# Two attention blocks on one core: x's columns for v requested half a set sooner and apart from their parts, sums kept open longer, some exponentials 1024 wide

## The chip, the cores and the metric

The kernel runs on one core of a Trainium2 chip. The metric is the device time of one execution in microseconds (us); lower is better. The runs of the kernel before gave 1745.47 us in the median (1745.34 to 1747.84, three runs).

## The reference, cut to what matters

Both halves take x (2048 x 640), wqkv (640 x 1920) and wo (640 x 640), all float32, with 32 heads of 20. A is a sliding window of 8 keys with a stride of 2; B is full attention. The outputs stand side by side.

```python
def _A_ref(x, wqkv, wo):                     # W, dil = 8, 2
    qkv = (x @ wqkv).reshape(B, S, 3, H, Dh).transpose(2, 0, 3, 1, 4)
    q, k, v = qkv[0], qkv[1], qkv[2]
    idx = arange(S)[:, None] - arange(W)[None, :] * dil
    ...
    attn = softmax(where(mask, einsum("bhsd,bhswd->bhsw", q, kg) * scale, -1e9))
    o = einsum("bhsw,bhswd->bhsd", attn, vg)
    return o.transpose(0, 2, 1, 3).reshape(B, S, D) @ wo

def _B_ref(x, wqkv, wo):
    ...
    p = softmax(einsum("bhqd,bhkd->bhqk", q, k) * Dh ** -0.5)
    o = einsum("bhqk,bhkd->bhqd", p, v)
    return o.transpose(0, 2, 1, 3).reshape(B, S, D) @ wo
```

## The kernel before, in words

**Numbers in two parts.** Products in fp32r keep fewer bits, so a value that enters one is cut into a first part (a rounded copy, `hi`) and a second part (value minus first part, `lo`), and a product is made of three passes (`PASSES`). `split` asks for the raw value by a DMA on SP's queue and makes both parts some ticks later: the copy on ScalarE, the difference on VectorE or, with `second=gp`, on GpSimd. A tick is a step of the program text (`tick`); `after(n, fn)` puts an instruction n ticks later into the queues. All queues run in program order.

**The stages.** First the projections of A to q and k (up to about 220 us), then those of B (up to about 281 us); both are stored in DRAM. Then the stage for v: 15 blocks and a remainder. Set c = 0 to 3 are 512 columns of A's x, c = 4 to 7 of B's; block 2c + half multiplies set c by one half of wv. From block 2 on, a matmul uses 64 rows, two run side by side, and after each pair of rows a `v_tick` follows, which also issues one `b_max` (two maxima 1024 wide) of B, loads of bq, and work of A's attention on GpSimd. `x_load(c + 2, 4)` at the end of block (c, 1) asks for the set after next and makes its parts four ticks later; `x_load(1, 5)` stands behind the first v group of block 0. `w_load` does the same for B's wv. Results go through ScalarE's copies to `ro` (four buffers) and by DMA to va_d, or to vb_d for B.

**The main loop.** B is cut into 32 units u (8 groups of 4 heads, 4 query quarters) of 16 key blocks each, 512 steps i. A step holds four halves of scores S (key rows against 512 queries), whose exponentials ScalarE makes from PSUM to SBUF (`s_exp`), four halves of maxima for a later step on VectorE, and the product of v with the exponentials (`b_pv`). The order is written out by hand in the string `ORDER`: a letter is a token, the digits its PSUM banks (eight banks of 128 x 512):

- S: two halves of scores, an exponential each. M: two halves of maxima, one reduction 1024 wide over two neighbouring banks. N: the same with two reductions of 512. Y: one half of scores and one of maxima.
- V: the product of step i - 2, with a digit if it opens a bank for the sum. Before, a sum covers two steps: the first V opens it, the second closes it. ScalarE then copies the sum to SBUF, and from the second sum of a unit on GpSimd adds the copy (`more`) to the unit's total (`braw`). The four buffers of `more` are the two tiles `spare`.
- H: a piece of A's output projection in two banks; j: a transpose of A's output on VectorE.

A's attention runs on GpSimd beside all this (`a_work`), paced by an estimate of GpSimd's time. The last 24 steps (`TAIL`) and B's output projection follow the loop.

The two lines that the change to the sums turns on are these:

```python
        n, part = divmod(kb, 2)
        ...
                      start=(part == 0), stop=(part == 1))
```

Of the kernel before, what the change touches and what calls it, by code (L numbers as in the profile page):

```python
# [75 lines left out]
def attention_pair(ctx, tc, xa, wqk_a, wv_a, wo_a, xb, wqk_b, wv_b, wo_b, oa, ob):  # L76
# [648 lines left out]
    accs, raws, spare = {}, {}, []  # L725
# [29 lines left out]
    def b_pv(i):  # L755
        u, kb = divmod(i, NKB)
        g, qc = divmod(u, NQC)
        n, part = divmod(kb, 2)
# [22 lines left out]
    def b_two(what, ns, one):  # L781
# [36 lines left out]
    def take(kind):  # L818

        m = None  # L820
        if kind == "S":
# [14 lines left out]
    def b_token(kind, ns):  # L836

        what, m = take(kind)
        b_two(what, ns if len(ns) == 2 else (ns[0], ns[0] + 1), kind == "M")
# [85 lines left out]
    def x_load(c, w):  # L925

        x, pieces = x_pieces((xa, xb)[c // 4], c % 4, gp)
        XV.append((x, pieces))
        wait[0] = w
        for fn in pieces:  # L930
            fn()
# [8 lines left out]
    for block in range(15):  # L940
        c, half = divmod(block, 2)
        s0 = c % 4 * 4
        if block < 2:
            for s in range(s0, s0 + 4):
                v_group(c, half, s)
                v_tick(2.2, False)
                if (block, s) == (0, 0):
                    x_load(1, 5)
        else:
            ps4 = [bank() for _ in range(4)]  # L950
            for second in range(2):
                for u in range(2):
# [45 lines left out]
    def begin(i):  # L998
# [29 lines left out]
        "Y07M1S36Y54V0Y71S26M4Y03V7Y06M4S31Y72V0Y13M4S76VY71M2S64S05N17V6Y04M2S51VY70M4S13S26N07V1Y25S04N36VY07S25M3Y61"  # L1028
        "V0Y72M3S56VY75M1Y63S04V5Y06M1S74VY07S64M1Y35V0Y74S16Y23VM4S73Y61V2jY70M4S31VY07Y63M4S12S70Y63jV1jS72jM4Y03VM6"
        "S52Y40V3Y71jM5S24VY70M1S46S35Y07V4S31jM6Y52VY03S71Y65jM3S02Y57V1jM3S06Y72VjM3S05Y26V7Y01M3jS56VY05M1S36Y47V5"  # L1030
        "Y03M1S64VY07S64S31N25Y70V6jM4S32M0VS75M3S26jY01jV7jY25M3S61VY02S65M3jS71V0Y26M3S75VY71Y26H54Y30H54S71H54Y62H54"
        "Y73H54M1Y06V3Y74M1S05VY07M4S61Y23V7Y60S15N42VN06S51H43Y27H43Y05H43Y61Y27H43H43M5Y01V2Y73S04M5VY70M3Y15S62V0Y17"
        "M3S62VY71M5S24Y30V1Y27M5S43VY07H23N46S15H23Y70H23Y14H23Y56H23M0Y74V5S63M0Y72VS63Y74N01V2Y36S05Y74VM0S36Y54V7"
        "Y03M1S64VN06S53H42Y71H42Y05H42Y36Y71H42Y05H42Y36V7Y02M4S63VS06M2Y14V7M5S03Y21VM3S05Y62V1Y07M3S25VY07M5S42H31"
        "H31Y07H31Y24Y56H31Y07H31M4S26V0Y71S23M4VY71M2S46Y50V1Y74S26N35VY07S62M3H51H51Y07H51Y62M3H51Y07H51N62V0S17M3S56"
        "VM1S75Y43V6Y70S51M2VY70S15M2Y46V0S71jM2Y54VS71jY26S35N40V7jN64S21Y03VM5S42Y10V3jY47M5jS02VY70M1S64S53N07V6Y52"
        "S01M3VY70M1S53S46N07V5Y41M2S06VY70Y61S42Y35S07Y61N45V2Y01M3S75VY07S16M3S52N07V1S63M4Y02VY73S04M5Y21V7Y03M5S42V"
        "Y04M2S15Y76V0S15M2Y74VS15Y76Y23V0Y14S56N73VY71Y24H56Y03H56S71H56N42S03H56H56N74S01V2Y37M5S04VY70S13M5Y42V0Y17"
        "S63N54VY71M5S23Y40V1Y72S36N54VY07M5S23Y41V7Y02S63N54VN06S51H23Y74H23Y05H23Y16Y74H23Y05H23Y16V7Y02M4S63VY06S13"
        "M4Y27V6S01jM4S32jVjM0S75Y43V2jY01M6S35jVS01M3S57N62V0S13S45M6VM1S34Y76V5Y03S21N46VY70M2S14S65N07V1Y26S03M4VY07"  # L1040
        "M2S64S51N70V6Y52M3S71VY70M1Y53S46Y07V5Y64M1S03VY07M3S62S51Y07V6Y52S43N71VY70M4S32Y16V0Y73M4S21VY73M1S64H50H50"
        "Y73H50Y46Y12H50Y73H50S41N62V7Y06S53Y42VM5S03Y21V4Y05M6S31VS05M2Y71S64V0M2S75Y16VM2S74Y56V1Y07M2S46VY07S64M2Y51"
        "V7Y06M2S45VY06M4S13H27H27Y60H27N13S45H27Y60H27S14N53V6Y75M1S03VY70S54M1Y36V0S75jM1jS43jVjM6S51Y24V3jY07M5S14V"
        "Y70M1S46S53N07V4Y56M1S03VY07M5S31S42N70V3S41M5S72VM0S74Y56V2Y73M0S46VY73S45M0S62N37V4Y05S36M1VY07M5S31S42N70V3"
        "Y41M5S72VY70M1S46S35N07V4S36M1S05VM6S03Y21V5Y04M6S13VY04M1S73H65H65Y04H65N73S21H65Y40H65S72N13V4Y05M6S31VY05"
        "S32M6Y14V5Y03S67Y21VM3S07Y61V2Y03M4S17VY03S16M4Y72V3Y01M4S67VS02M6S15Y43V0M6S12Y35VM6S14H52Y30H52Y16Y74H52Y30"
        "H52Y16H52M3Y70V1S25M6Y43VY02M6S54Y31V0Y24M6S53VY15M3S27Y06V5jS12jM3jS70jVM1S67Y34V0jY12M5S74VY71M2S46Y50V1Y74"
        "M2S65VY07M5S42S31N70V4Y35M6S21VY05M1S37S64N50V3Y27S16M4VY70M1S64S35N07V6Y41M2S05VS70M4S13Y26V7Y01M4S63VY06S12"
        "Y35Y47Y60N15V2S70S34N16VM0S73Y65V4Y70M1S35VY07S63M1H54H54Y07H54Y63Y21H54Y07H54M2S61V0Y74S56M2VY71S64M2S50V1M6"
        "S24Y35VM6S02Y54V3Y07M1S46VN07S64H51Y23H51Y06H51Y74Y23H51H51M6Y04V2Y31S07M5VY01M3S75Y62V1Y07M3S56VS07M5S24Y31V0"  # L1050
        "M5S72Y14VM5S72Y34V1jY07S26M4VjY07M2S64S51jY70jV6jM2S54Y01VM2S74Y50V1Y27M3S06VY07S62M3S51N70V6Y52M3S71VY70M1S53"
        "S46N07V5Y41M2S06VY70Y61M2S45Y07V6Y51M2S04VY70Y15S42M6S03N15V4Y07S62Y31VM6Y05S12V3S40M6Y51VS02M6S54Y13V0Y72S65"
        "M3VY71Y62H34Y50H34S71H34N26S50H34H34M1S75V6Y04M1S73VY70S54M1Y36V0Y75Y14S23VM6S51Y24V3Y07M5S14VY70S12M5Y43V0Y71"
        "M5S24VY71M2S46H50H50Y17H50Y64Y32H50Y17H50M3Y62V1S07M5Y43VY07M5S42Y31V0Y72M5S43VY74M1S36Y05V4Y37M1S60VM6S05S31j"
        "Y24jV0jM6S53Y14VY75M2jS61jV4Y05M6S32VY05M2S17S46N50V1Y72M4S36VY07M2S64S51Y07V6Y52M3S71VN70S52M3S16Y75V0Y12M3"
        "S67VY12M6S53S40Y21V5M6S41Y03VM6S41Y23V0Y74M5S13VY71M3S25S60N17V2Y36M4S01VY07S16S35N42N70V1S26Y34Y75VY02Y36H45"
        "H45Y72H45Y60Y31H45Y72H45S06N31V7Y52M3S01VS06M1S35Y47V0M1S36Y75VY14S23M5V7Y04S12M5VY04S13M5S27V4M0S35Y62VN70S15"
        "H23H23M6S41H23Y05H23H23M6N41S05V2S03M6Y54VS03Y15S76N24V0Y15M2S74VY71S65M2V4jY70S61M2VjY07M5S13S24jY70V1jM5S23"
        "Y04VjM5S72Y34V0Y17S26Y54VM1S73Y46V5Y70M1S63VY07S64M1S35N70V6Y14M2S75VY70M4S13S26N07V1Y25M3S06VY07Y62S53S41Y70"
        "N62V5Y60S43M1VY07M1S36Y45Y70V3Y42S15M6VY04M1S57Y63V4Y50M1S76VY07M5S31Y24V7Y03S61N52VY06S15M3H27H27Y60H27N15S34"  # L1060
        "H27Y60H27S13M4V6S70M1S54VY70M1S35V4Y07S63M1VY07S65M1Y34V7Y06S51M2VY06M4S13Y27V6Y01M4S32VY70M2S14H56H56Y70H56"
        "Y41Y23H56Y70H56M1Y43V7S06M4Y12VY06S15M3Y27V0S16jM3Y52VS71jM3S56Y20V7jM3S51Y06VjM3S52Y16V0Y75M3jS26VY71S26M3Y50"
        "V1Y27S63M4VY07M2S64S51N70V6Y52M3S71VS70M1S53Y46V7Y05M1S36VY03S45Y61Y27Y30N41V5S06S72M3VM0S76Y43V2Y70S15N36VY70"
# [123 lines left out]
```

## Time and profile before

| what | value |
|---|---|
| median of the runs | 1745.47 us |
| profiled execution, its own time | 1745.1 us |
| span of its instructions | 1742.9 us |
| granted TensorE clock, mean | 0.998 |
| busy PE / VectorE / ScalarE / GpSimd | 1726.1 / 1349.3 / 1337.3 / 1271.9 us |
| v stage, about | 281 to 463 us |
| main loop, about | 463 to 1628 us |

Busy time of an engine is the union of its instructions. ScalarE's and VectorE's instructions overlap their neighbours a little, so the mean length of one times the count is more than the busy time. In a row of the timeline, the first number is the start, the second the length of all the instructions merged in it (their count stands behind x), and square brackets give the idle time of the engine ahead of it and what ended that.

### The profile page before, as it was taken

The page shows a single profiled execution, that of the slowest core. Times are in us where ns is not written, and L with a number is a line of the kernel's source. Part 1 is how long each engine was busy: PE and PEld are TensorE (multiplying, and loading weights), DVE is VectorE, ACT ScalarE, POOL GpSimd, SP SyncE. Part 2 cuts the span into 40 slices and gives each one's busy share as a digit, 9 for nine tenths or more (in the row PEclk, how much of TensorE's full clock was granted, in tenths as well). Part 3 has the DMA queues.
Part 4 walks back from the last instruction along what each step waited for, and adds up shares of the span by engine and source line. Part 5 has one row for each costly group of instructions (what it writes and reads, how often), then busy time and mean ns, then how long its engine had stood idle before and what let it go on. Part 6 is the DMA issues. An engine that isn't in the chain of part 4 may idle for free.

```text
span 1742.9 us, 34666 instructions
## 1 busy us (share of the span) xinstructions
PE 1726.1 (99%) x12711; PEld 1011.2 (58%) x12711; DVE 1349.3 (77%) x1818; ACT 1337.3 (77%) x2658; POOL 1271.9 (73%) x1125
## 2 busy tenths in 40 slices
PE   9999999999999999999999999999999999999999
PEld 8988888989635544444444443444444445444568
DVE  3113232888899999999999999999999999999300
ACT  4323223232599999999999999999999999999981
POOL 0000950999899999999999999999999953545242
PEclk9999999999999999999999999999999999999999
DMA  6447878657754263445435433543642532111123
GB/s 226 120 139 242 304 258 261 219 183 219 207 152 133 91 175 119 130 127 148 128 121 158 141 126 106 176 136 110 168 137 96 142 90 55 43 36 52 34 75 113
DMA packets 194435, 248.29 MB, mean 142 GB/s; under 512 B 89308, under 2 KB 114396, under 8 KB 193272
## 3 DMA queue, kind: packets, MB, share of 16 engines
q1 hardware_dynamic: 193688, 245.41, 46.6%
q8 instruction: 100, 1.64, 0.4%
q14 instruction: 71, 0.58, 0.1%
q10 hardware_dynamic: 576, 0.66, 0.1%
HBM read 181.08 MB, written 64.91 MB: 141 GB/s over the span
## 4 chain that ended last, share of the span: by engine, by line
PE 73%; POOL 17%; DMA 4%; issue 3%; DVE 2%; ACT 1%; SPq 1%; POOLq 0%; ACTq 0%; DVEq 0%
PE ps_st L71 73%; POOL akv L71 9%; POOL braw L71 4%; DVE mx L71 2%; POOL ao L71 1%; DMA stg<-xa 1%; SPq L71 1%; DMA mdr<-mtr 1%; DMA bq<-qb_d 1%; POOL ww L71 1%; POOL al L71 1%; ACT e L71 1%; DMA s_d<-braw 1%; POOL xn L71 0%; DMA s_d<-sm 0%
## 5 line engine op out<-in xcount | busy, mean ns | idle before, releaser
L71 DVE TENSOR_REDUCE mx<-ps_st 128x1 f32<-128x512 f32 (+1 forms) x1500 | 1227.5, 877 | 72.5 <-PE ps_st L71 61.4
L71 ACT ACTIVATE e<-ps_st 128x512 f32<-128x512 f32 x2048 | 1067.3, 630 | 32.5 <-PE ps_st L71 19.6
L71 PE MATMUL ps_st<-bk,bq 60*128 60x512 f32 x2048 | 555.1, 436 | 0.5 <-DVE mx L71 0.4
L71 PE MATMUL ps_st<-bq,bk 62*128 62x512 f32 x2048 | 548.7, 431 | 3.5 <-ACT e L71 1.8
L71 PE MATMUL ps_st<-e,vb 128*32 128x512 f32 x4096 | 543.1, 604 | 0.5
L71 PEld LDWEIGHTS ps_st<-bq,bk 62*128 62x128 f32 x2048 | 276.6, 184 | 401.6 <-ACT e L71 250.2
L71 POOL TENSOR_TENSOR braw<-braw,more 128x512 f32<-128x512 f32 x224 | 288.3, 1287 | 85.6 <-ACT more L71 85.1
L71 PEld LDWEIGHTS ps_st<-bk,bq 60*128 60x128 f32 x2048 | 257.9, 184 | 102.9 <-DVE mx L71 45.1
L71 POOL TENSOR_TENSOR akv<-akv,aq 128x1280 f32<-128x1280 f32 x64 | 188.4, 2944 | 166.4 <-DMA akv<-ka_d 166.3
L71 POOL TENSOR_TENSOR akv<-akv 128x640 f32<-128x640 f32 (+3 forms) x304 | 282.6, 930 | 14.7
L71 ACT COPY ro<-ps_st 128x320 f32<-128x320 f32 (+2 forms) x172 | 73.9, 465 | 185.9 <-PE ps_st L71 104.0
L71 PE MATMUL ps_st<-ww,xn 64*128 64x320 f32 (+1 forms) x1776 | 188.1, 311 | 6.5 <-POOL xn L71 2.4
L71 PEld LDWEIGHTS ps_st<-ww,xn 64*128 64x128 f32 (+1 forms) x1776 | 175.6, 187 | 22.6 <-ACT e L71 8.3
L71 PEld LDWEIGHTS ps_st<-e,vb 128*32 128x32 f32 x4096 | 82.2, 108 | 149.9 <-issue 77.1
L71 POOL TENSOR_TENSOR akv<-akv,al 128x1280 f32<-128x1280 f32 x64 | 151.6, 2368 | 0.1
L71 ACT COPY more<-ps_st 128x512 f32<-128x512 f32 x224 | 136.7, 610 | 4.0 <-POOL braw L71 2.0
L71 PE MATMUL ps_st<-xn,w 128*128 128x512 f32 x480 | 115.8, 390 | 0.0
L71 PEld LDWEIGHTS ps_st<-xn,w 128*128 128x128 f32 x480 | 90.1, 188 | 19.4
L71 POOL TENSOR_TENSOR xn<-stg,xn 128x512 fp32r<-128x512 f32 (+1 forms) x30 | 53.8, 1804 | 62.8 <-ACT xn L71 61.5
L71 PE MATMUL ps_st<-ww,aot 64*128 64x320 f32 x960 | 99.2, 308 | 0.0
L71 ACT CAST pr<-ps_st 128x512 fp32r<-128x512 f32 x40 | 23.5, 587 | 98.7 <-PE ps_st L71 93.0
L71 PEld LDWEIGHTS ps_st<-ww,aot 64*128 64x128 f32 x960 | 91.0, 186 | 4.6 <-DVE mx L71 0.5
(65 smaller groups left out, 1042.3 us busy)
## 6 DMA issues: line engine op xcount, KB each, us to landing
akv<-ka_d SPq DMA_DIRECT2D x128, 320.0 KB
akv<-va_d SPq DMA_DIRECT2D x128, 320.0 KB
kb_d<-pr SPq DMA_DIRECT2D x20, 512.0 KB
qb_d<-pr SPq DMA_DIRECT2D x20, 512.0 KB
bk<-kb_d SPq DMA_DIRECT2D x16, 640.0 KB
bq<-qb_d SPq DMA_DIRECT2D x64, 160.0 KB
stg<-xb SPq DMA_DIRECT2D x16, 512.0 KB
rb<-s_d SPq DMA_DIRECT2D x128, 64.0 KB
```

The source lines that it names most:

```text
L71: return self.tc.keep_in_program_order(op(*a, **k))
```

## The change

What it does:

1. `x_load` is cut in two. `x_raw(c)` only asks for the three raw pieces, into buffers of the ring `p`; `x_parts(c, raws, second)` makes the parts at once. `x_raw(1)` is issued in the last pair of projections of B, behind the fourth load of bq; its parts are made behind the fourth v group of block 0, with the second parts on VectorE, and `x_raw(2)` follows there. The later sets are requested after the first tick of block (c, 1) and cut into parts at its end.
2. `w_load(0, 9)` becomes `w_load(0, 8)`.
3. `load_out(wo_a, ...)` makes its second parts on VectorE; those of wo_b stay on GpSimd.
4. In `ORDER` two letters are new. v is a V that leaves the sum open, so that a sum can cover one to five steps. T is an S whose two exponentials are one instruction over two neighbouring banks. The whole string is another one: 330 S, 254 T, 784 Y, 409 M, 119 N (before 627 S, 698 Y, 444 M, 127 N), and 225 sums are closed in it (before 243). H, j and the steps are as many as before.

```diff
+    def x_raw(c):
+        out = []
+        for a, b in PAIRS:
+            t = sb.tile([128, 1024], F32, tag="p", bufs=PB, name="stg")
+            raw = t[:, :(b - a) * 512].rearrange("p (k c) -> p k c", c=512)
+            sp.dma_start(raw, (xa, xb)[c // 4][a * 128:b * 128, c % 4 * 512:c % 4 * 512 + 512].rearrange("(k p) c -> p k c", p=128))
+            out.append((a, b, raw))
+        return out
...
                     elif g8 == 6:
                         for _ in range(4):
                             q_loads.pop(0)()
+                        xraw = x_raw(1)
...
-    def b_pv(i):
+    def b_pv(i, keep=False):
...
-        n, part = divmod(kb, 2)
+        part = int(u in accs)
...
-                      start=(part == 0), stop=(part == 1))
+                      start=(part == 0), stop=not keep)
...
-        if part == 0:
+        if keep:
             return
         del accs[u]
+        n = sums[u] = sums.get(u, -1) + 1
...
-            if kind == "s":
+            if kind == "s" and not one:
                 s_exp(i, j, r, psb[:, n])
-            elif not one or r == 1:
+            elif kind == "s" and r == 1:
+                s_exp(i, j, slice(0, 2), psb[:, n - 1:n + 1])
+            elif kind == "m" and (not one or r == 1):
...
-    def x_load(c, w):
...
+    def x_parts(c, raws, second=gp):
+        t = columns(c % 4)
+        XV.append((t, None))
+        for a, b, raw in raws:
+            u, m = t[a // (KC - 1)], a % (KC - 1)
+            hi, lo = (u[:, x, m:m + b - a] for x in range(2))
+            act.copy(hi, raw)
+            second.tensor_tensor(lo, raw, hi.bitcast(F32), ALU.subtract)
...
-                if (block, s) == (0, 0):
-                    x_load(1, 5)
+                if (block, s) == (0, 3):
+                    x_parts(1, xraw, dve)
+                    xraw = x_raw(2)
...
                     v_tick(V_US)
+                    if half and c < 6 and not second and not u:
+                        xraw = x_raw(c + 2)
...
-            w_load(0, 9)
+            w_load(0, 8)
         if half:
             if c < 6:
-                x_load(c + 2, 4)
+                x_parts(c + 2, xraw)
...
-            w, more = wide_pieces(src[h], gp)
+            w, more = wide_pieces(src[h], *((dve, gp.tensor_copy) if src is wo_a else (gp,)))
...
-        "Y07M1S36Y54V0Y71S26M4Y03V7Y06M4S31Y72V0Y13M4S76VY71M2S64S05N17V6Y04M2S51VY70M4S13S26N07V1Y25S04N36VY07S25M3Y61"
+        "Y07M1Y36N54V0Y71M5M2S04V7Y06T2M4Y71v0Y26M4S73VY71M2S64Y05Y17v6Y02M3S51VY70M1S53N46S07v5S03M1S47vY60M3T1VY07M1"
...
-                b_pv(i - LAG)
+                b_pv(i - LAG, kind == "v")
...
-            b_pv(i - LAG - 1)
+            b_pv(i - LAG - 1, True)
             b_pv(i - LAG)
```

More of the change, by code (lines that the diff above doesn't have):

```diff
@@ L724, in attention_pair @@
     P = {}
-    accs, raws, spare = {}, {}, []
+    accs, raws, sums, spare = {}, {}, {}, []
     def s_matmul(i, pl, r, p):
@@ L820, in take @@
         m = None
-        if kind == "S":
+        if kind in "ST":
             what = [s_half(), s_half()]
@@ L838, in b_token @@
         what, m = take(kind)
-        b_two(what, ns if len(ns) == 2 else (ns[0], ns[0] + 1), kind == "M")
+        b_two(what, ns if len(ns) == 2 else (ns[0], ns[0] + 1), kind in "MT")
         if m:
@@ L923, in v_tick @@
         a_pace(v_us[0])
-    def x_load(c, w):
[L927 to L931, printed above, removed]
+    def x_parts(c, raws, second=gp):
[6 more added lines that the diff above has]
+            second.tensor_tensor(lo, raw, hi.bitcast(F32), ALU.subtract)
     def w_load(half, w):
@@ new lines, in attention_pair @@
+        "S02v1S04Y56Y72vY06T4M2VY07M4Y63T1v7Y06S54M1VjY06T4M1jS37jv0jT4jM1Y36VY75M1T3Y60V7Y53Y42H16Y07H16S53N42H16S07"
+        "H16Y54H16M2Y07v4Y56M2S01VY07M5T2Y14v7Y03T5M1VY03Y46T1N57v3Y04S56M1VY07H65Y41M2H65S70H65Y41H65H65M2Y70Y14v6T2"
+        "Y75N01VS25Y74N03v6T4M1S70vjT4jM1jS73jvjY05S74M1VY70T4M1Y36V0Y75Y41H23Y60H23Y75H23Y41H23Y07H23M4Y61V0Y72S36Y54"
+        "N01v7S62M3Y05VY61S02M3Y57v6Y02S13M4VY70H12N35S46H12Y07H12Y34H12M5Y07H12V3Y04M5Y71T2v4Y07S56M2VY70T5M2Y14v0M5"
+        "Y73T1VN74T5T1N30V7M5T3Y21v0Y73M5S42VY71S24H35N06H35S71H35Y02H35Y46H35M1Y07V6Y53M1Y04T6v5Y03S21M6VY04M2T6Y15v4"
@@ L1088, in attention_pair @@
+        "v7Y14T5M2VY04Y15T2M6Y40v1Y25T6M3VY02M6S53S41N20v5Y46M2S71VY07Y61T2M4Y70v6Y13M4S72VY70M2S14S56N07v1Y25M3S06VY07"
+        "Y62T3Y51Y70v6N41T2Y05vY74T2N01VY70S52M3S16N07v5Y41M2S06VY70Y61T2M4Y07v6Y13M4S02VY70Y13T4Y62N07v1Y25T3Y06vY72T3"
+        "M5VY07M3S25S61N70v2Y36M4S71VY07Y16T4Y32Y70v1N26T4Y03vY27T4N06VY07Y25T3Y61v7Y05T1N34VN03S65T1Y47N06v3S72Y01M4V"
+        "Y72M0Y64Y53S72v6S75M0Y24VY75M0S23S46N75v2Y01T3Y76vY01T3Y56vY01T3M6VM0T3M6S52")
     owed = []
@@ L1095, in attention_pair @@
     i = 0
-    for kind, *ns in re.findall("[A-Zj][0-7]*", ORDER):
+    for kind, *ns in re.findall("[A-Zjv][0-7]*", ORDER):
         ns = [int(n) for n in ns]
@@ L1102, in attention_pair @@
             out_owed()
-        elif kind != "V":
+        elif kind not in "Vv":
             b_token(kind, ns)
```

107 lines of the change are left out of this document (48 added, 59 removed).

## The prediction, made before the changed kernel ran

> **What bounds the kernel now.** I read the page's span first, then windows by stage, then the waits of PE's weight loads in the main loop, and last the timeline around the places where PE stood. A row of the windows has the stretch and its length, the busy time and instruction count of PE, PEld, DVE, ACT and POOL, the granted clock, the DMA share and GB/s.
>
> ```profile
> span 1742.9 us, 34666 instructions
> ```
>
> ```profile
> 298.70:305.90 7.20, 2.62 (x18) 1.79 (x16) 0.00 (x0) 3.49 (x6) 4.75 (x3) 0.75 0.80 285
> 305.90:309.00 3.10, 3.10 (x20) 2.93 (x22) 0.13 (x1) 0.00 (x0) 2.94 (x5) 0.50 0.95 335
> 463.00:1628.00 1165.00, 1160.53 (x8624) 528.20 (x8624) 1133.05 (x1584) 1130.19 (x2266) 1014.78 (x895) 1.00 0.42 119
> ```
>
> ```profile
> PEld ps_st L71 <- ACT e L71: 335.9, 537, 2.8
> PEld ps_st L71 <- DVE mx L71: 160.5, 334, 0.9
> PEld ps_st L71 <- issue: 88.3, 284, 0.8
> ```
>
> In the main loop (463 to 1628 us: nearly all exponentials, most maxima and products with v) PE is busy 1160.53 of 1165 us, but that is not proof of a bound: matmuls overlap, and one that runs late is still drawn as running. VectorE is busy 1133.05 us there and ScalarE 1130.19, 97% each. VectorE's idle 31.95 us is the most that a better order alone can win. Of the 584.7 us that weight loads waited in the three rows, 335.9 (57%) ended with an exponential and 160.5 (27%) with a maximum. So ScalarE and VectorE hold the loop together, and ScalarE is more often the one that releases PE. The other place is 298.7 to 309: PE is busy 2.62 of 7.20 us, and then works at clock 0.50.
>
> **The change, part by part.** The sum is made against the profiled execution: span 1742.9, execution 1745.1 us, which is 0.4 under the median 1745.47 of the runs.
>
> (1) The second set of x's columns (c = 1) is asked for behind the fourth load of bq, in the last projection for q and k, and not after the first v group; its second parts go from GpSimd to VectorE. The chain, ScalarE, PE and VectorE of before at this place:
>
> ```profile
> 279.71 11.17 DMA bq<-qb_d
> ...
> 290.92 6.25 DMA stg<-xa
> ```
>
> ```profile
> 299.70 0.43 ACT L71 COPY ro<-ps_st 128x320 f32<-128x320 f32 x1 [4.90 <-DMA va_d<-ro]
> 300.02 1.99 ACT L71 CAST xn<-stg 128x1024 fp32r<-128x1024 f32 x2
> ```
>
> ```profile
> 298.31 0.60 PE L71 MATMUL ps_st<-ww,xl 128*128 128x320 f32 x3
> 301.12 0.41 PE L71 MATMUL ps_st<-ww,xn 64*128 64x320 f32 x2 [2.21 <-ACT xn L71]
> 303.56 1.97 PE L71 MATMUL ps_st<-ww,xn 64*128 64x320 f32 x12 [2.02 <-POOL xn L71]
> 305.87 1.70 PE L71 MATMUL ps_st<-ww,xn 64*128 64x320 f32 x10 [0.35 <-POOL xn L71]
> ...
> 309.03 1.96 PE L71 MATMUL ps_st<-ww,xn 64*128 64x320 f32 x24
> ```
>
> ```profile
> 308.87 2.36 DVE L71 TENSOR_REDUCE mx<-ps_st 128x2 f32<-128x1024 f32 x2 [20.08 <-PE ps_st L71]
> ```
>
> And a tick (one call of v_tick and the v matmuls ahead of it) in the regular course, with the place of part (3) behind it:
>
> ```profile
> 368.49 1.92 PE L71 MATMUL ps_st<-ww,xn 64*128 64x320 f32 x24
> ...
> 371.21 0.46 PE L71 MATMUL ps_st<-ww,xn 64*128 64x320 f32 x4
> 372.90 1.14 PE L71 MATMUL ps_st<-ww,xn 64*128 64x320 f32 x12 [1.23 <-POOL ww L71]
> ...
> 376.02 1.92 PE L71 MATMUL ps_st<-ww,xn 64*128 64x320 f32 x24
> ```
>
> Block 1 ends at 298.31 + 0.60 = 298.91 and the second tick of block 2 begins at 309.03: 10.1 us for a tick that costs 371.21 - 368.49 = 2.7. So 7.4 us are lost: 2.21 wait for x's first parts from ScalarE, 2.02 and 0.35 for the second parts from GpSimd, and the rest because PE runs at 0.50 afterwards. The request now stands right behind the loads of bq that begin at 279.71, some 9 us before 290.92. If x lands even at 295.5, the casts (two in 1.99 us and a smaller one) and VectorE's parts end by about 299, an estimate; VectorE stood idle for 20.08 us here, so its work costs nothing. Late next are ScalarE's copies to ro: each needs a buffer that a store to va_d must free (4.90 us of waiting at 299.70), those stores now stand behind x in SP's queue, and block 2 needs all four banks that the copies of block 1 free. I leave half of 4.90, 2.4 us, to them and take **-5.0**. Ends: -7.4, and +2.4 (two further waits of 4.90 in place of the 7.4).
> [...]
>
> (2) Sets 2 to 7 are asked for three ticks ahead of the end of a set, and cut into parts at that end and not a block (four ticks) later. Three ticks are 8 us; x took 6.25 to land. The parts are the same work, one block earlier.
>
> ```profile
> 357.47 0.76 ACT L71 COPY ro<-ps_st 128x320 f32<-128x320 f32 x2 [7.39 <-issue]
> ```
>
> ScalarE stands for 7.39 us between copies in these blocks, which hides its casts; GpSimd's order changes, its work doesn't. If a set is still on its way, ScalarE stands in front of the copies that free banks, and SP's stores to va_d and loads of akv stand behind the request: bounds 0 and a late landing of 2 us (8 against 6.25 and as much again) for one set. I take **0**.
>
> (3) wv_b's first half is cut a tick sooner, and x's parts no longer lie right ahead of it on GpSimd:
>
> ```profile
> 371.31 3.88 POOL L71 TENSOR_TENSOR ww<-stg,ww 128x640 fp32r<-128x640 f32 x3
> ```
>
> PE waited 1.23 us for ww, and its tick from 371.21 took 4.8 where 2.7 is regular. GpSimd reached ww only at 371.31; one tick sooner and without x's parts ahead it has at least 2.7 us to spare for PE's first need. I take **-2.1**; ends -2.1 and 0, if GpSimd's other work fills the place.
>
> (4) wo_a's six second parts go from GpSimd to VectorE.
>
> ```profile
> 286.83 1.96 DVE L71 TENSOR_TENSOR ww<-stg,ww 128x640 fp32r<-128x640 f32 x3 [3.79 <-ACT ww L71]
> ```
>
> ```profile
> 490.49 0.58 ACT L71 COPY more<-ps_st 128x512 f32<-128x512 f32 x1 [1.98 <-POOL braw L71]
> ...
> 491.63 0.50 PE L71 MATMUL ps_st<-bq,bk 62*128 62x512 f32 x1 [1.85 <-ACT e L71]
> ```
>
> Three such parts took VectorE 1.96, so six 3.9. GpSimd, late with ww and then braw, held ScalarE's copy 1.98 us and PE through it 1.85; that goes (-1.9). VectorE has 3% idle to hide 3.9, so I put half on the path. Together **0**; ends -1.9 and +2.0.
>
> (5) The order. Counting its letters: pairs of exponentials go from 627 S to 330 S and 254 T (one exponential of 1024); maxima from 444 M, 127 N and 698 Y to 409, 119 and 784; closed sums from 243 to 225. PE's matmuls stay the same in number.
>
> ```profile
> L71 ACT ACTIVATE e<-ps_st 128x512 f32<-128x512 f32 x2048 | 1067.3, 630 | 32.5 <-PE ps_st L71 19.6
> L71 DVE TENSOR_REDUCE mx<-ps_st 128x2 f32<-128x1024 f32 x548 | 661.8, 1216 | 44.8 <-PE ps_st L71 42.7
> L71 DVE TENSOR_REDUCE mx<-ps_st 128x1 f32<-128x512 f32 x952 | 615.0, 682 | 27.7 <-PE ps_st L71 18.7
> ...
> L71 ACT COPY more<-ps_st 128x512 f32<-128x512 f32 x224 | 136.7, 610 | 4.0 <-POOL braw L71 2.0 <-PE ps_st L71 1.5 <-issue 0.3
> ...
> L71 ACT CAST xn<-stg 128x1024 fp32r<-128x1024 f32 x30 | 30.7, 1053 | 4.5 <-DMA stg<-xa 4.2 <-DMA stg<-xb 0.3
> ```
>
> ```profile
> 700.82 3.11 ACT L71 ACTIVATE e<-ps_st 128x512 f32<-128x512 f32 x6
> ```
>
> ScalarE: 18 copies fewer at 136.7 / 224 = 0.61 are 11 us. An exponential of 1024 is not in this trace. Alone, by the cast of that width, it takes 1053 ns against twice 630: 0.207 us less. In a run of six the starts lie (3.11 - 0.63) / 5 = 0.50 apart and in a run of two casts 1.99 - 1.05 = 0.94: 0.06 less than two exponentials. The exponentials do run in rows, but from PSUM, so I take half of the nearer end, 0.03 each: 8 us for 254 (ends 0 and 53). ScalarE gains 19, and PE sees its 57%: -11. VectorE: 35 M fewer at 661.8 / 548 = 1.208 against 70 halves more (86 Y, less 16 of N) at 615.0 / 952 = 0.646: +2.9, in full on the path. Banks: a T frees its first bank at 1.053 and not at 0.630, 0.42 later. By the letters the banks of a T are asked for again after 4.47 tokens on average, those of an S before after 4.21; a token of the loop lasts 1165 / 1896 = 0.61, which gives 0.16 back. The other 0.26, 254 times, is 66 us of 8 x 1165 bank-us, under 1%; I price it at +2. GpSimd's 18 adds less are hidden, since it held PE only in (4). The loop: -11 + 2.9 + 2 = **-6**. Ends: -25 (VectorE's idle 31.95 less its 2.9 and 3.9 of work) and +21 (rival E).
>
> [...]
>
> Sum: 1745.1 - 5.0 - 2.1 + 0 + 0 - 6 = **1732**.
>
> **The rivals.**
> A, the forecast: 1732, its own range 1726 to 1738.
> B: a T saves what one alone shows, and the order turns that into time until VectorE's work is the floor: -25 for -6, so 1713, or 1720 with a third of it left. For it: 57% of the waits end with ScalarE. Against: rows of exponentials show only 0.06.
> C: the request for x does not do its work, because it queues behind the loads of bk and bq (the bq of 279.71 took 11.17 us to land): (1) is 0, and the time 1737.
> D: VectorE alone sets the loop. ScalarE's relief is then worth nothing, and VectorE's 2.9 and the 2.0 of (4) are paid: 1745.1 - 7.1 + 2.9 + 2.0 = 1743, with 1739 to 1747. For it: VectorE is as full as ScalarE. Against: PE waits for it half as often.
> E, slower: banks that a T returns late stop PE. All first banks together come 254 x 0.42 = 107 us later; if a fifth of that is on the path, the loop is +21 and not -6, with -7.1 before it 1759; with an eighth (13 us) 1751. It decides from (7.1 + 3.5) / 107, one T in ten, if nothing of ScalarE's relief arrives. For it: 41% of the tokens of S, T, Y, M and N (38% before) stand in an open sum, with seven banks left. Against: the longer distance in the letters.
>
> **How the numbers follow.** A 0.38, B 0.13, C 0.11, D 0.17, E 0.21. A change of less than 0.2% (3.5 us) can't be told from none here. Faster (under 1742.0) are A, B, C and a third of D: 0.68. The same (to 1749.0): most of D, 0.10. Slower: E and a rest of D, 0.22. The range leaves out half of B and half of E: 1716 to 1753.
>
> **What would show it.** (1) is right if PE no longer waits for ACT xn or POOL xn around 299 to 309 and the clock stays at 1.00; wrong if such a wait stays, or if ACT ro waits over 5 us for va_d. (3): no PE wait for POOL ww. (4): no ACT more behind POOL braw near 490. (5): ScalarE some 20 us less busy in the loop, VectorE within 8 of 1133, an exponential of 1024 near 1.05 and its successor 0.95 later. The prediction is wrong towards B if VectorE idles under 15 us in the loop; towards D if ScalarE is relieved and the loop still takes 1165; towards E if PE's waits that end with ACT e grow.

## The result and the profile after

The changed kernel takes 1769.38 us in the median (1769.19 to 1771.7), beside 1746.26 for the kernel before on the same chip: a ratio of 1.0134, 95% interval 1.0117 to 1.0152. It is 23 us slower where 13 us faster was forecast, and 10 us above the slowest time that any case of the prediction named (1759). Its profiled execution took 1771.7 us. Numbers in brackets, (1) to (5), are the steps of the prediction.

The rows that answer to those of the prediction: the span, the windows of the two places and of the loop (stretch, length, busy time of PE, PEld, DVE, ACT, POOL, granted clock, DMA share, GB/s), then the waits of PE's weight loads in the loop, then the two shapes of exponentials.

```profile
span 1769.9 us, 34595 instructions
```

```profile
298.70:305.90 7.20, 6.21 (x73) 5.75 (x75) 2.64 (x4) 1.28 (x3) 0.00 (x0) 1.00 0.85 245
472.10:485.75 13.65, 5.61 (x24) 1.52 (x24) 6.97 (x9) 2.28 (x4) 5.37 (x9) 0.50 0.68 212
526.70:533.50 6.80, 6.61 (x27) 1.89 (x27) 3.33 (x5) 4.89 (x10) 6.57 (x5) 0.50 0.63 190
465.80:1655.50 1189.70, 1166.57 (x8626) 515.09 (x8624) 1138.00 (x1623) 1115.03 (x1997) 982.15 (x867) 0.99 0.41 116
```

```profile
PEld ps_st L71 <- ACT e L71: 315.0, 492, 0.9
PEld ps_st L71 <- DVE mx L71: 179.7, 354, 10.4
```

```profile
L71 ACT ACTIVATE e<-ps_st 128x512 f32<-128x512 f32 x1540 | 831.0, 614 | 47.1 <-PE ps_st L71 38.1 <-ACT e L71 0.3
...
L71 ACT ACTIVATE e<-ps_st 128x1024 f32<-128x1024 f32 x254 | 263.5, 1039 | 14.0 <-PE ps_st L71 12.7 <-ACT e L71 0.2
```

The first place is mended: PE is busy 6.21 of 7.20 us from 298.7 (2.62 before), at clock 1.00. ScalarE is relieved too: its busy time over the whole span falls from 1337.3 to 1321.4. And yet the loop takes 24.7 us more: from the first product of v with the exponentials to that of step 486 it lasts from 465.8 to 1655.5, 1189.7 us, and from 463.0 to 1628.0, 1165.0 us, before. The v stage ends 2.8 us later instead of sooner, and what follows the loop is 0.5 shorter: 2.8 + 24.7 - 0.5 = 27.0, the difference of the spans (1769.9 - 1742.9). These are the profiled executions; the medians lie 23 us apart.

The loop does not lose evenly. PE stands in a few places, and the waits tell of it: the longest wait for DVE mx is 10.4 us (last number of its row), where it was 0.9. The first is at 470, in the timeline of after (start, length, engine, operation, and in brackets the idle time ahead and its end):

```profile
459.02 0.33 SPq L71 DMA_DIRECT2D stg<-wo_a  x1
...
476.24 0.72 POOL L71 CAST ww<-stg 128x640 fp32r<-128x640 f32 x1 [3.82 <-DMA stg<-wo_a]
...
476.99 0.82 DVE L71 TENSOR_TENSOR ww<-stg,ww 128x640 fp32r<-128x640 f32 x1 [7.61 <-POOL ww L71]
...
480.14 0.79 PE L71 MATMUL ps_st<-bq,bk 62*128 62x512 f32 x1 [9.97 <-DVE mx L71]
```

Read it from the end. PE stands 9.97 us for maxima that free its banks. VectorE runs four of them in a row at 479.41, and none sooner: ahead of them in its queue stands a difference for wo_a, which waits 7.61 us for its first part on GpSimd, which waits 3.82 us for wo_a. This piece was asked for at 459.02 and landed just before 476.24, some 17 us later. Nothing in the loop needs wo_a yet. From 472.10, while PE still stands, its clock is at 0.50, for 13.65 us.

The second kind is at 524 and at 956:

```profile
524.96 1.26 POOL L71 TENSOR_TENSOR braw<-braw,more 128x512 f32<-128x512 f32 x1
...
526.25 0.58 ACT L71 COPY more<-ps_st 128x512 f32<-128x512 f32 x1 [2.65 <-POOL braw L71]
...
526.89 1.29 PE L71 MATMUL ps_st<-bk,bq 60*128 60x512 f32 x3 [2.31 <-ACT more L71]
```

```profile
956.75 0.58 ACT L71 COPY more<-ps_st 128x512 f32<-128x512 f32 x1 [4.94 <-POOL braw L71]
...
957.39 0.79 PE L71 MATMUL ps_st<-bq,bk 62*128 62x512 f32 x1 [4.51 <-ACT more L71]
```

ScalarE's copy `more` waits until GpSimd has read the previous copy out of the same buffer (it begins when the add at 524.96 is over), and all exponentials stand behind that copy. `spare` has four buffers, but they are chosen by the number of the sum within its unit, and begin anew with each unit. Before, every unit had eight sums and so seven copies, and a buffer came round after three copies or more. Now the letters give units of 6 to 9 sums. Where a unit has six there are five copies, and the last one and the first one of the next unit fall on the same buffer. That happens three times; the third of these stops, at 879, took 1.15 us.

The later end of the v stage has a stop of its own, at 329. VectorE waits for GpSimd's `al`, which A's softmax needs, and PE's maxima stand behind that:

```profile
330.59 0.58 DVE L71 TENSOR_REDUCE am<-al 128x32 f32<-128x256 f32 x1 [4.47 <-POOL al L71]
...
332.37 0.80 PE L71 MATMUL ps_st<-bk,bq 60*128 60x512 f32 x2 [3.45 <-DVE mx L71]
```

### The profile page after: what moved, and what is told of

The parts are those of the page before. It is cut to its first block, busy times and chain, and to the rows that moved or that the text cites. A ratio compares the mean times of both kernels' runs of the same rounds, so it can differ in the third digit from the quotient of the medians.

```text
span 1769.9 us, 34595 instructions
## 1 busy us (share of the span) xinstructions
PE 1733.3 (98%) x12711; PEld 998.6 (56%) x12711; DVE 1358.8 (77%) x1862; ACT 1321.4 (75%) x2386; POOL 1238.6 (70%) x1098
## 4 chain that ended last, share of the span: by engine, by line
PE 81%; POOL 7%; DVE 6%; DMA 4%; issue 1%; SPq 0%; ACT 0%; POOLq 0%; ACTq 0%
PE ps_st L71 81%; DVE mx L71 6%; POOL akv L71 4%; POOL braw L71 1%; DMA bq<-qb_d 1%; DMA va_d<-ro 1%; DMA stg<-wo_a 1%; POOL ao L71 1%; DMA bk<-kb_d 1%; POOL xn L71 0%; SPq L71 0%; POOL ww L71 0%; POOL al L71 0%; DMA stg<-xa 0%; DVE am L71 0%
## 5 line engine op out<-in xcount | busy, mean ns | idle before, releaser
L71 ACT ACTIVATE e<-ps_st 128x512 f32<-128x512 f32 (+1 forms) x1794 | 1049.6, 674 | 61.1 <-PE ps_st L71 50.7
L71 PE MATMUL ps_st<-bq,bk 62*128 62x512 f32 x2048 | 560.1, 436 | 18.1 <-DVE mx L71 11.1
L71 PE MATMUL ps_st<-bk,bq 60*128 60x512 f32 x2048 | 569.3, 437 | 7.6 <-DVE mx L71 4.8
L71 PEld LDWEIGHTS ps_st<-bq,bk 62*128 62x128 f32 x2048 | 270.0, 185 | 447.9 <-ACT e L71 249.9
L71 POOL TENSOR_TENSOR braw<-braw,more 128x512 f32<-128x512 f32 x206 | 265.1, 1287 | 108.8 <-ACT more L71 107.8
L71 PEld LDWEIGHTS ps_st<-bk,bq 60*128 60x128 f32 x2048 | 267.0, 185 | 87.6 <-DVE mx L71 35.5
L71 ACT COPY more<-ps_st 128x512 f32<-128x512 f32 x206 | 123.2, 598 | 14.8 <-POOL braw L71 9.7
L71 PE MATMUL ps_st<-ww,aot 64*128 64x320 f32 x960 | 103.5, 313 | 0.2 <-DVE mx L71 0.2
L71 POOL TENSOR_TENSOR xn<-stg,xn 128x512 fp32r<-128x512 f32 (+1 forms) x28 | 49.1, 1763 | 67.3 <-PE ps_st L71 66.0
```

Source lines behind the costliest of these rows:

```text
L71: return self.tc.keep_in_program_order(op(*a, **k))
```

## The experiments

Two theories. **S**: the loss is a few stalls, instructions that wait at the head of a queue which others need, and each has a place in the text from which it can be moved; without them the order is worth something like what was forecast. **O**: the new order itself is slower (banks, or VectorE's halves), and the stalls are a minor part. A time in brackets is the kernel before on the same chip; each ratio is against that.

**The three parts of the change, taken back one at a time, then together.**

e1_wo_gp, in the changed kernel:

```diff
+    gq = InOrder(tc, nc.gpsimd)
-  *((dve, gp.tensor_copy) if src is wo_a else (gp,))
+  *((gq, gp.tensor_copy) if src is wo_a else (gp,))
```

(gq is GpSimd without its pacing estimate.)

> Part (4) alone undone: wo_a's six differences are GpSimd's again, all else as in the changed kernel (GpSimd's pacing estimate too). Theory S (VectorE's program order: a difference that waits for wo_a's landing stands ahead of maxima): PE's stop of 9.97 us at 470 goes, and with it the 13.65 us at half clock, a loss of some 11 to 13 us in all: 1757 to 1759 us. Theory O (the new order itself is slower, through 1024 wide exponentials and long sums): the stop was only drawn in one place, the time stays within 4 us of 1769.4.

e2_ring, in the changed kernel:

```diff
-            more = spare[n % 2][:, n // 2 % 2]
+            mores[0] += 1
+            more = spare[mores[0] % 2][:, mores[0] // 2 % 2]
```

> The four buffers of more are taken in turn over all units, not by the number of the sum within its unit; all else as in the changed kernel. Theory S: with units of six sums the old rule takes the same buffer for two copies in a row (three times in the string), and ScalarE's copy, and PE behind it, waits for GpSimd's addition: PE's stops of 2.3, 1.15 and 4.5 us at 524, 878 and 952 and two falls of the clock go, 8 to 12 us: 1757 to 1761. Theory O: GpSimd's lag is the same, the stops move to other sums, the time stays within 4 us of 1769.4.

e3_x_old puts `x_load` back with its places, and `w_load(0, 9)`; the rest stays.

> Parts (1), (2) and (3) undone: x's columns are asked for and cut as before the change, wv_b too. Theory S: the loop of the changed kernel began 2.9 us later than before in spite of the wait for x that went; with the old course it begins near 463, so about 3 us less: 1765 to 1768. If asking sooner were a gain and the later start came from GpSimd alone, the time rises by up to 5.

e4_all3 has all three edits: of the change only the order, with T and the longer sums, is left.

> All three together: the parts (1) to (4) as before the change, the buffers of more in turn, and only the order with v and T left of the change. Theory S: the three losses add up and the order is worth nothing or a few us: 1740 to 1747. Theory O: the order costs 10 us or more by itself: 1755 or above.

Measured: e1 took 1763.13 (1745.66), ratio 1.0102 (1.0087 to 1.0117); e2 1758.54, 1.0078 (1.0063 to 1.0093); e3 1768.34, 1.0136 (1.0121 to 1.0151); e4 1750.31, 1.0031 (1.0018 to 1.0044). Against after that is -6.2, -10.8, -1.0 (which lies within the intervals) and -19.1. The two stalls are 17 of the 23 us, as S says. e2's time lies in the range that S gave it. But e1 gave half of what S expected, and its trace says why. The stop at 470 is gone, GpSimd has six differences more to do, and so comes later to the add that the copy waits for:

```profile
516.87 0.59 ACT L71 COPY more<-ps_st 128x512 f32<-128x512 f32 x1 [5.42 <-POOL braw L71]
...
517.50 1.29 PE L71 MATMUL ps_st<-bk,bq 60*128 60x512 f32 x3 [5.06 <-ACT more L71]
```

The stop that took 2.31 us in after takes 5.06 here: a part of what was mended came back through the other fault. In e2 the waits of that copy for GpSimd over the whole span fall as they should; the first row is after's, the second e2's (engine and tile, what was waited for: us in total, times, longest):

```profile
ACT more L71 <- POOL braw L71: 9.7, 4, 4.9
```

```profile
ACT more L71 <- POOL braw L71: 0.5, 1, 0.5
```

e4, though, is still 4.6 us slower than before, between S (to 1747) and O (from 1755), so the order, freed of the two, does not bring its 6.

**Wide exponentials.** e5_count is e4 with wo_a wholly as before, so that GpSimd's pacing (`gp`) counts its six differences again:

```diff
-  *((gq, gp.tensor_copy) if src is wo_a else (gp,))
+  gp
```

> As e4 (only the order with v and T is left, the buffers of more in turn), but wo_a's differences on GpSimd are counted in its pacing estimate, as before the change, so that A's attention is put into the queues some 8 us later. Theory S (what e4 still lost, 5 to 8 us around 514 to 525, was GpSimd running behind the order at the loop's start): 1742 to 1747. Theory O (the order costs the 4.6 us of e4 by itself): 1749 to 1752.

e6_count_s is e5 with a T made as two exponentials of 512:

```diff
-            if kind == "s" and not one:
+            if kind == "s":
                 s_exp(i, j, r, psb[:, n])
-            elif kind == "s" and r == 1:
-                s_exp(i, j, slice(0, 2), psb[:, n - 1:n + 1])
```

> As e5, with each T made as two exponentials of 512 (an S): banks, sums and order the same. The prediction's step (5) gave a T 0.03 us of ScalarE's time and 2 us in all for later banks: by it this one is 2 to 4 us slower than e5. Rival E (a T's banks come back too late): this one is faster than e5 by 3 us or more. If neither matters: within 2 us.

e5 took 1761.22 (1746.53), 1.0087 (1.0073 to 1.0101); e6 1766.12, 1.0115 (1.0100 to 1.0131). e6 against e5: the wide exponentials save 4.9 us. From step 32 on, the windows of e5 and then e6 are 4.7 us apart, and ScalarE is busy 12.4 us less:

```profile
548.86:1638.33 1089.47, 1081.01 (x8039) 478.60 (x8037) 1054.99 (x1496) 1037.07 (x1857) 914.60 (x805) 1.00 0.40 114
```

```profile
552.18:1646.39 1094.21, 1086.73 (x8039) 487.70 (x8037) 1056.19 (x1496) 1049.52 (x2092) 915.48 (x804) 1.00 0.40 114
```

The rival by which T's late banks cost more than T saves is refuted: with T off, the kernel is slower. e5 itself missed both theories, 10.9 us above e4 with nothing changed but an estimate in the text. Its trace has two stops, each set by a wait of VectorE for GpSimd:

```profile
521.94 0.31 DVE L71 STREAM_TRANSPOSE turn<-ao 128x128 f32<-128x128 f32 x1 [6.28 <-POOL ao L71]
...
522.88 0.79 PE L71 MATMUL ps_st<-bq,bk 62*128 62x512 f32 x1 [6.32 <-DVE mx L71]
```

```profile
1294.87 0.59 DVE L71 TENSOR_REDUCE am<-al 128x32 f32<-128x256 f32 x1 [4.98 <-POOL al L71]
...
1296.11 1.94 PE L71 MATMUL ps_st<-e,vb 128*32 128x512 f32 x8 [5.67 <-DVE mx L71]
```

They are of the same kind as the one at 470: VectorE's transpose `turn`, or its maximum `am` for A's softmax, stands ahead of B's maxima and waits for GpSimd's `ao` or `al`. In e4 the first is there with 2.32 us and the second is not.

**The stage for v on the two orders.** e7_xnew is e5 with the requests and parts of x and wv as in the change.

> As e5, with x's columns and wv_b as in the changed kernel (parts 1 to 3). The prediction gave them -7.1 us. Theory S (the earlier parts stand ahead of A's attention in GpSimd's queue, VectorE and PE then wait for a softmax): 1 to 4 us slower than e5.

e7 took 1747.45 (1746.53), 1.0008 (0.9999 to 1.0017): not a little slower than e5, as was expected, but 13.8 us faster. Its loop begins 3.3 us later than e5's (466.8 against 463.5), and the wait of `turn` there is 2.02 us and not 6.28. A loop that starts later seems to give GpSimd time. That was not tested by itself, but it is plain that the parts of the change don't add up.

To see each part without this, three kernels are the kernel **before** with one edit. e8_b_wo has wo_a's differences on VectorE alone, with the pacing kept as it was; e9_b_x1 part (1) alone (the early request for set 1, its second parts on VectorE); e10_b_xnew parts (1) to (3).

```diff
 e8   -  w, more = wide_pieces(src[h], gp)
      +  w, more = wide_pieces(src[h], *((dq, gp.tensor_copy) if src is wo_a else (gp,)))
 e9   +  xraw = x_raw(1)                  # in the last projections of B
      -  x_load(1, 5)
      +  x_parts(1, xraw, dve)            # behind the fourth group of block 0
 e10  as e9, and
      +  xraw = x_raw(c + 2)              # after the first tick of block (c, 1)
      -  x_load(c + 2, 4)
      +  x_parts(c + 2, xraw)             # at its end
      -  w_load(0, 9)
      +  w_load(0, 8)
```

(dq is VectorE with the time added to GpSimd's estimate.)

> The kernel before with part (4) alone: wo_a's six differences on VectorE, GpSimd's pacing estimate unchanged. The prediction gave it 0 (-1.9 to +2.0). Theory S (a difference that waits for the landing of wo_a holds the maxima behind it): a stop of 5 to 10 us in VectorE and PE at 465 to 480 here too, 1751 to 1759. If the stop needs the new order's timing: within 2 us of before.

> The kernel before with part (1) alone: set 1 of x's columns asked for behind the loads of bq, cut behind block 0 with its differences on VectorE; sets 2 to 7 and wv_b as before. The prediction's step (1): PE's wait for x and the fall of the clock at 299 to 309 go, -5.0: 1740 to 1743, the main loop begins near 458. If ScalarE's copies behind x give it back: 1745 to 1748.

> The kernel before with parts (1), (2) and (3). The prediction: -7.1, 1738 to 1741. Theory S: cutting sets 2 to 7 a block earlier puts GpSimd's differences ahead of A's attention, VectorE's softmax maximum at 331 waits for GpSimd with PE's maxima behind it, and the gain of (1) is gone: the loop begins 2 to 4 us later than before, 1747 to 1751.

e8 took 1759.26 (1746.53), 1.0079 (1.0065 to 1.0094): the old order pays 12.7 us for six differences of 3.9 us. The first stop is that of after. At the second, VectorE doesn't wait, but two differences take it 4.18 us; the last section comes back to them:

```profile
473.39 0.83 DVE L71 TENSOR_TENSOR ww<-stg,ww 128x640 fp32r<-128x640 f32 x1 [6.24 <-POOL ww L71]
...
476.31 0.80 PE L71 MATMUL ps_st<-bk,bq 60*128 60x512 f32 x2 [8.38 <-DVE mx L71]
...
481.50 4.18 DVE L71 TENSOR_TENSOR ww<-stg,ww 128x320 fp32r<-128x320 f32 x2
...
486.34 0.80 PE L71 MATMUL ps_st<-bk,bq 60*128 60x512 f32 x2 [2.97 <-DVE mx L71]
```

e9 took 1741.75 (1746.16), 0.9973 (0.9962 to 0.9983): -4.4. Around 299, where PE lost 7.4 us, this is left:

```profile
298.92 0.41 PE L71 MATMUL ps_st<-ww,xn 64*128 64x320 f32 x1 [0.48 <-ACT ro L71]
...
300.29 2.81 PE L71 MATMUL ps_st<-ww,xn 64*128 64x320 f32 x23 [0.96 <-ACT ro L71]
```

0.48 and 0.96 us for banks that the copies to `ro` free: what the prediction named as late next, at 1.4 us in place of the 2.4 left for it. The clock still falls here; from 281 to 309 its mean is 0.94 in e9:

```profile
281.00:309.00 28.00, 26.56 (x212) 26.07 (x213) 10.71 (x13) 8.09 (x15) 0.00 (x0) 0.94 0.81 253
```

e10 took 1753.03, 1.0038 (1.0025 to 1.0050): 11.3 us slower than e9, by parts (2) and (3). e11_b_xmix is e10 with one thing taken back: sets 2 to 7 are still asked for sooner, but cut into parts at the old place.

```diff
-                x_parts(c + 2, xraw)
+                after(4, x_parts, c + 2, xraw)
```

> As e10, but sets 2 to 7 keep the old place of their parts (four ticks after the end of a set) and are only asked for sooner. Theory S (the place of the parts is what costs, not the request): as fast as e9 or up to 3 us faster, through wv_b: 1738 to 1743. If the early requests cost (SP's queue, the stores to va_d): as slow as e10.

e11 took 1740.26 (1746.16), 0.9963 (0.9950 to 0.9975): the lowest median here, with e9 within its interval. So of part (2) it was the earlier cut that cost, about 12.8 us. Some 7 us of that lie ahead of the loop, which begins at 464.5 in e10 and at 457.2 in e11. Another 4 lie in the loop, spread evenly over its first three quarters; what makes those is open. GpSimd's queue and what waits for it, in e10 and then in e11:

```profile
307.01 4.77 POOL L71 TENSOR_TENSOR xn<-stg,xn 128x1024 fp32r<-128x1024 f32 x2 [64.68 <-ACT xn L71]
...
312.98 0.47 POOL L71 TENSOR_TENSOR am<-al 128x128 f32<-128x128 f32 x1
...
329.27 0.58 DVE L71 TENSOR_REDUCE am<-al 128x32 f32<-128x256 f32 x1 [4.44 <-POOL al L71]
...
331.04 0.79 PE L71 MATMUL ps_st<-bk,bq 60*128 60x512 f32 x2 [3.44 <-DVE mx L71]
```

```profile
242.43 0.47 POOL L71 TENSOR_TENSOR am<-al 128x128 f32<-128x128 f32 x1
...
312.94 4.78 POOL L71 TENSOR_TENSOR xn<-stg,xn 128x1024 fp32r<-128x1024 f32 x2 [57.79 <-ACT xn L71]
```

```profile
329.64 0.61 DVE L71 TENSOR_REDUCE am<-al 128x32 f32<-128x256 f32 x1
```

In e10 set 2's differences were put into GpSimd's queue early. They couldn't run before 307, as the data had not come, and GpSimd stood 64.68 us with A's softmax work (`am`) behind them. In e11 that work was put in first, and GpSimd did it at 242, in a time when it had nothing else; the differences ran at 312.94, early enough. VectorE's `am` then waits for nothing, where in e10 it waited 4.44 us and PE 3.44. In the kernel before, the differences of set 1 stand ahead of that work in the same way, but its VectorE comes to that step only at 335.5, as PE has lost its 7.4 us by then, and GpSimd is done. By these times, what part (1) wins brings VectorE there too soon for the early cut.

Part (3) shows in the same stage. In after, the first half of wv_b is cut at 368.22 and PE no longer waits for it. But PE now waits for the second half, since the early cut puts a set of x right ahead of that one on GpSimd:

```profile
384.29 1.28 POOL L71 TENSOR_TENSOR xl<-stg,xl 128x512 fp32r<-128x512 f32 x1
...
385.53 3.88 POOL L71 TENSOR_TENSOR ww<-stg,ww 128x640 fp32r<-128x640 f32 x3
...
387.11 1.14 PE L71 MATMUL ps_st<-ww,xn 64*128 64x320 f32 x12 [1.80 <-POOL ww L71]
```

From 340 to 465 PE waits 2.2 us for ww in after, 1.9 in before, and 0.2 in e11, where it waits 1.4 for xn instead.

**Is the order itself slower?** e12_n_x1 is e5 with part (1) alone, on the new order.

> The new order with the buffers of more in turn and wo_a's differences on GpSimd, as e5, and part (1) alone of x's. If e5's two stops (6.3 us at 516 behind a transpose that waits for GpSimd, 5.7 us at 1290 behind a softmax maximum) come from where A's attention happens to fall in the order, they change with GpSimd's 6 us less in the estimate: 1740 to 1748, as e7. If they belong to e5's way of counting: e5 less 5, 1755 to 1758.

e12 took 1754.57 (1746.16), 1.0050 (1.0037 to 1.0063), 6.7 faster than e5 and just under the 1755 to 1758 of the second case: its two stops, 7.12 and 5.93 us, are no shorter than e5's. e14_n_soft changes two numbers in it, the distance at which A's `am` steps follow GpSimd's work in VectorE's queue:

```diff
-        job(soft_jobs, 5, lambda: dve.tensor_reduce(...))
+        job(soft_jobs, 8, lambda: dve.tensor_reduce(...))
-        job(soft_jobs, 5, lambda: dve.reciprocal(...))
+        job(soft_jobs, 8, lambda: dve.reciprocal(...))
```

> The kernel with the new order, the ring, wo_a as before and the early request for set 1 (1754.57), with one number changed: VectorE's two steps of A's softmax (the maximum over the window and the reciprocal) are put into the queue eight ticks and not five behind GpSimd's work that they wait for. Theory S (VectorE stands in front of its maxima for GpSimd): the stop near 1284, which ended with VectorE's am, goes, and perhaps part of the one near 510: 6 to 11 us less, 1744 to 1749. Theory O: GpSimd is as late as before, the stop moves to the next thing that waits for it (turn, aot or braw), and the time is within 3 us of 1754.57.

e14 took 1748.07 (1746.04), 1.0013 (1.0004 to 1.0022): -6.5. The wait of `am` in e12, and the same in e14:

```profile
1288.92 0.59 DVE L71 TENSOR_REDUCE am<-al 128x32 f32<-128x256 f32 x1 [5.24 <-POOL al L71]
...
1290.16 1.93 PE L71 MATMUL ps_st<-e,vb 128*32 128x512 f32 x8 [5.93 <-DVE mx L71]
```

```profile
1289.40 0.62 DVE L71 TENSOR_REDUCE am<-al 128x32 f32<-128x256 f32 x1 [1.12 <-POOL al L71]
```

The wait is 1.12 us for 5.24, and PE no longer stands there. Finally e13_n_xmix, the changed kernel with all three mends (e1's, e2's, and e11's late cut):

> The changed kernel with three of its steps mended at once: the copies go through the four spare buffers in turn, wo_a's second parts are GpSimd's again (not counted in its pacing), and sets 2 to 7 are asked for sooner but cut into parts at the old place. The new order and the early request for set 1 stay. Theory S (the loss is the stalls; the order itself is worth about what it won from step 32 on): the v stage should end near 457 us as in the kernel before with the same x, against 464.4 with the old x, and the loop should be that of the run with the old x (464.4 to 1629.3): about 1743, that is 1740 to 1747, and the two stops near 515 and 521 as there, under 2.5 us each. Theory O (the new order puts GpSimd behind, wherever the loop starts): the sooner start is eaten by longer stops around 510 and 1284, and the time is 1749 to 1757, as the early request for set 1 alone gave in the kernel with the pacing as before.

e13 took 1745.81 (1746.04), 0.9997 (0.9989 to 1.0006): no difference to before, 23.6 us under after. The loop in three stretches of steps, counted from 0 by the start of their product of v, before's rows first (0 to 15, 16 to 31, 32 to 484; windows as above):

```profile
463.00:499.90 36.90, 35.05 (x246) 13.78 (x246) 34.78 (x51) 34.20 (x69) 31.03 (x29) 1.00 0.58 165
499.90:539.70 39.80, 38.77 (x285) 17.08 (x284) 37.92 (x59) 38.86 (x79) 39.17 (x31) 1.00 0.58 162
539.70:1623.20 1083.50, 1082.89 (x8078) 495.76 (x8078) 1056.04 (x1470) 1052.33 (x2111) 943.07 (x834) 1.00 0.41 116
```

```profile
457.10:492.20 35.10, 35.03 (x249) 13.76 (x247) 34.12 (x53) 34.24 (x62) 30.77 (x30) 1.00 0.66 194
492.20:541.60 49.40, 44.77 (x323) 20.19 (x321) 40.92 (x64) 39.80 (x72) 48.06 (x41) 0.93 0.60 148
541.60:1624.10 1082.50, 1079.27 (x8038) 477.60 (x8036) 1054.43 (x1496) 1036.73 (x1857) 914.96 (x805) 1.00 0.41 115
```

In the first stretch the new order wins 1.8 us. In the second it loses 9.6, and PE is busy only 44.77 of 49.40 at clock 0.93: here GpSimd is behind in e13 as well,

```profile
513.96 0.31 DVE L71 STREAM_TRANSPOSE turn<-ao 128x128 f32<-128x128 f32 x1 [2.82 <-POOL ao L71]
...
514.90 0.79 PE L71 MATMUL ps_st<-bq,bk 62*128 62x512 f32 x1 [2.80 <-DVE mx L71]
```

and VectorE (`turn`) waits 2.82 us for it, with B's maxima behind; ScalarE (`al`) waits 2.36 us at 507. Over the remaining 453 steps the order wins 1.0 us, though ScalarE is busy 15.6 us less (1036.73 for 1052.33) and VectorE 1.6 less. That is the answer to S and O: the loss of after is stalls, S. But e11 has the same treatment of x on the old order and took 1740.26, so as a whole the new order still costs some 5.6 us: what it wins elsewhere doesn't make up for steps 16 to 31. And from step 32 on it is worth 1 us and not 6. In that O was nearer. Whether e14's distance, put into e13, would bring it under e11 was not tried.

## Why the prediction was wrong

**(1)** was right: -4.4 alone (e9) for -5.0, and what came late next was the copies to `ro`. One reading of before was coarse: the prediction has PE at clock 0.50 after the 7.20 us from 298.70. In two halves of 3.60 us each, that stretch has the clock at 0.99 up to 302.30 and at 0.50 from there, so the fall came near 302.3, when PE had stood 2.21 us and 0.7 of the next wait.

**(2)**, taken at 0 with bounds of 0 and 2, failed, by the sentence "GpSimd's order changes, its work doesn't". The order is what costs: a difference that must wait, put ahead of A's softmax in GpSimd's queue, made VectorE and through it PE stand. Parts (2) and (3) together cost 11.3 us on the old order (e10 against e9), and asking sooner without cutting sooner costs nothing (e11). The changed kernel has the same stop, 3.45 us at 332, which with its fall of the clock (0.50 from 332.13 for 6.83 us) ate what part (1) had won. Its bounds looked at ScalarE's queue and SP's, and GpSimd's was named and then left.

**(3)**, taken at -2.1, failed by its own sign, "no PE wait for POOL ww": the wait for the first half (1.6 of the 1.9 us) went, and with (2) one of 2.2 came for the second half. The sentence "x's parts no longer lie right ahead of it on GpSimd" looked at the first half alone. With the late cut (e11) the wait moved to the set of x behind it, 1.4 us, so little of the 2.1 could come; the gain over e9, 1.5 us, lies within the intervals.

**(4)**, taken at 0 with 2.0 as its upper end, cost 12.7 us on the old order and 6.2 in the changed kernel. The failed step is the price: 3.9 us of VectorE's busy time, half of it hidden. What counted was the wait of the moved instruction. Before, the differences waited for wo_a in GpSimd's queue, where what stood behind them was in no such hurry; in VectorE's the maxima stood behind them, and each of those frees a bank. The trace of before has wo_a asked for at 455.27, behind the loads of bk in SP's queue, and its first cast at 471.61, but the prediction did not ask how late it lands. At the stops of this change, what stood behind a waiting instruction of ScalarE or VectorE waited with it, the longest with 9.97 us of PE.

**(5)**, taken at -6, failed in two steps; the order alone cost 4.6 us (e4). "GpSimd's 18 adds less are hidden" looked at their time only; the adds moved nearer to the copies that reuse their buffers, 10.8 us (e2), and the longer sums were the cause. The formula for `more` should have been followed for the new counts. And "PE sees its 57%" of ScalarE's relief: 15.6 us of relief brought 1.0 us from step 32 on (e13). The share of waits that end with an exponential is no rate of exchange. When exponentials come sooner, other things end the waits: over the same steps 32 to 484, the waits of PE's weight loads that end with ACT e fall from 311.4 us before to 293.7 in e13, those with DVE mx grow from 146.3 to 158.0, and those with issue, where the profile shows nothing waited for, from 80.4 to 100.8. This fits rival D's mechanism, VectorE as the floor, which had 0.17; no run tested it by itself. For T alone the result came out right by luck: 8 us x 57% is 4.6, and e6 against e5 shows 4.9. But ScalarE's relief was 12.4 us there and not 8, and 4.7 of it arrived, 38% and not 57%. The copies' 11 us were mis-sized the other way: with the T's made as S (e6), ScalarE is busy 1049.52 us against 1052.33 before in these steps, 2.8 us less. Why the copies gave so little, and what the banks take, is open.

Rival E had the right sign with the wrong cause: banks of T. That an instruction waiting in a queue stops the instructions behind it stood in the bounds of (2), for ScalarE and at 2 us; none of the five cases was built on it, and it happened in three places of one change (with 9.97, 4.51 and 3.45 us of PE at the longest stop of each).

Most of these stops were not paid by their length alone: with those of 9.97, 4.51, 3.45 and 2.31 us in after, the clock was at 0.50 for 6.8 to 13.65 us. The last section has more on that.

## What to carry to other kernels

When an instruction moves to another engine or to an earlier place in a queue, price first what it will wait for and what stands behind it there; its busy time comes second. Put an instruction that waits for a transfer or a slow engine where the queue behind it is in no hurry, or far enough behind its producer: a distance of eight ticks instead of five, or a cut four ticks later, was worth 6 to 13 us here. When the number of items per round changes, follow every index that begins anew with the round; and a share of waits says which engine released last, not how much time comes back when that engine gets faster.

## What was not expected of the hardware

Short stops of PE came with a lower clock here. In the rows of the section on the result the clock is at 0.50 for 13.65 us at the stop of 9.97, 5.6 of them after its end, and for 6.8 from the end of the stop of 2.31. After, near the end of the stop of 4.51 at 956, and around the one of 1.15 at 879:

```profile
956.80:963.60 6.80, 6.21 (x37) 5.73 (x37) 2.69 (x5) 4.97 (x11) 1.42 (x1) 0.50 0.81 148
876.00:884.00 8.00, 6.85 (x62) 4.64 (x60) 6.79 (x11) 6.09 (x13) 7.84 (x8) 1.00 0.22 68
```

Again 6.8 us at 0.50, and none for the stop of 1.15. With the stop of 3.45 at 332 it is 6.83, from 332.13. The stop of 1.80 at 385 in after has none: the mean clock from 380 to 395 is 1.00, with PE idle for 2.18 us. In e9 the mean from 281 to 309 is 0.94, with PE idle for 1.44 us in two stops, of 0.48 and 0.96. So neither the longest stop nor the idle time tells here whether the clock falls; what does was not shown. In five of these seven places a stop cost its length and a stretch at a lower clock with it.

An exponential of 1024 columns takes 1039 ns in after and one of 512 takes 614. By their lengths one wide instead of two saves 0.19 us, but neighbours overlap: the 1540 of 614 ns, 945.6 us by their lengths, keep ScalarE busy for 831.0. In e5 against e6, 254 wide ones relieved ScalarE by about 0.05 each (12.4 us from step 32 on), and the kernel by 0.019 (4.9 us).

Two differences on VectorE ran much longer while GpSimd worked. Where GpSimd stood still, one of 128 x 640 took 0.82 us and one of 128 x 320 took 0.485 (at 286.83 and 288.3 in before). In e8 the two at 481.50, one of 128 x 320 and, by its cast at 479.80, one of 128 x 640, took 4.18 us together, while GpSimd ran an instruction of 2.92 from 481.16 and one of 0.98 from 484.02. That the two engines hinder each other here is a guess of the author's; no run tested it, nor did the price of (4) count on it.
